# A key load in halves, mixer tiles in other rounds and a wait left out, in a gated attention and mixer decode kernel

## The chip, the core and the metric

One core of a Trainium2 chip runs the kernel. The metric is device microseconds of one execution, median of several runs. The core has a tensor engine (PE), a vector engine (DVE), a scalar engine (ACT), GpSimd (POOL) and a sync engine (SP), each with its own instruction stream; they wait for each other by semaphores. SP issues nearly all the loads here, into one queue that 16 DMA engines work off in order.

## What is computed

One token is decoded. Its 16 query heads, in groups of two, attend over 8 cached key and value heads of 65536 positions and 256 channels; beside this a small token mixer (a layer norm and an MLP with tanh GELU) runs on the same token, and a sigmoid gate mixes the two results. All tensors are bf16.

```python
def _A_ref(x, k_cache, v_cache, wq, wo):
    q = (x @ wq).reshape(B, Sq, 16, 256) ...
    scores = jnp.einsum("bhqd,bhkd->bhqk", q, k) * (Dh ** -0.5)
    p = softmax(scores)
    return jnp.einsum("bhqk,bhkd->bhqd", p, v) ... @ wo
def _B_ref(x, w1, b1, w2, b2):
    h = layernorm(x)                                   # [1, 1, 448]
    u = gelu(jnp.einsum("bsd,sf->bdf", h, w1) + b1)    # [1, 448, 1792]
    return (jnp.einsum("bdf,fs->bds", u, w2) + b2).transpose(0, 2, 1)
g = sigmoid((x * gate_w).sum(-1, keepdims=True))
return g * a + (1 - g) * b
```

The key and value caches are 268 MB each and are read once.

## The kernel before

The cache is worked off in `NP` = 32 rounds, called pairs in the change's title: four rounds (`PPH`) for each of 8 key heads. A round covers 16384 positions: 8 MB of keys and 8 MB of values. It consists of 8 chunks (`BODY`) of 2048 positions; the first four (`DC`) lie in one half of the round's keys, the last four in the other. In what follows K5 and V5 are the keys and values of round 5.

**PE, one round** (loop at L515). It first finishes the running maximum of the round before (`maxima`, L382 and L384). Then come the keys (`keys`, L371): for chunk k, 16 transposes into PSUM (`kst`, L344), interleaved with the scores of chunk k-1 (L365). DVE copies the even quarters of `kst` out to `ktT` (L650), ACT the odd ones (L787); a chunk's transposes wait until the chunk before it is copied out (`sem_ev`, L342). Before chunk 0 PE waits for the round's keys (`sem_k`, L333), before chunk 4 for `sem_kb` and, in rounds 2 and 3 alone, for a second half that came as a load of its own (`sem_kc`, L336 to L338, each under an `If`). Before the keys of a round it also waits for `s_qc` (L527), which DVE raises each time that it has copied the query of a head to `qcur` (L713, L735). After the keys come the mixer's projection if a tile is ready (L538) and `values` (L401 on): the exponentials `pT` of the round before times its values, 128 matmuls at L396. So round j multiplies the values of round j-1 (round 2 skips this, rounds 0 and 1 use their own), and round index 32 does the last ones. Every fourth round a head is finished: cleared, turned and multiplied by its part of `wo` (L446, L457).

**DVE, one round** (L722): 8 chunk copies; every fourth round the end of a head (`finish_head`); the maximum (L656 to L679); and in rounds 0 to `FT` - 1 = 13 one of 14 mixer tiles (`mixer`, L625 to L643), twelve operations on 128 x 448 with ACT's tanh (L791) between them. At the end of a head DVE copies the next query (L735). Since an engine's stream runs in order, the mixer tile of round j stands before the chunk copies of round j+1.

**SP's queue** (L282 to L306). The keys have a ring of one and a half rounds, `kring`; the values have one buffer, `vbuf`. K of round j is issued when PE has transposed the first four chunks of round j-1 (`sem_tr`, L287). V of round j is issued when the values of the round before are multiplied (`sem_pv`), since it overwrites their buffer. Loads of a round are one DMA of 8 MB each, except those of the first rounds: K0, K2 and K3 come in halves. The last values, V31, come in five pieces: the first (56 of 128 slices, 3.5 MB) goes to a free part of `kring`, the others wait for the multiplication of V30 (L305); behind them stand two last loads of `wo`.

**The end** (`tail`, L415 on): the pieces are multiplied as they land, the last ones already turned; the head is divided, projected and written out.

Of the kernel before, what the change touches and what calls it, by code (L numbers as in the profile page):

```python
# [7 lines left out]
AF = mybir.ActivationFunctionType  # L8
# [4 lines left out]
def bass_gated_mix__gqa_block_cached__mixer_token_mlp__decode_kernel(  # L13
# [22 lines left out]
    REP = HQ // H  # L36
    F = B_w1.shape[1]
    FT = F // 128
# [10 lines left out]
    NC = H * NCPH  # L49
    BODY = 2 * DC  # L50
    NV = BODY * NT
    NP = NC // BODY
    PPH = NCPH // BODY
# [10 lines left out]
    LEAD = 2  # L64
# [12 lines left out]
    GC0 = 0.796875  # L77
    GC1 = 0.044677734375

    assert FT <= NP - PPH  # L80

    HV = NV // 2
# [10 lines left out]
    with ctx:  # L95
# [6 lines left out]
        def new_sem(name):  # L102
            return ctx.enter_context(nc.semaphore(name))
# [90 lines left out]

        sem_k = new_sem("sem_k")
        sem_kb = new_sem("sem_kb")
        sem_kc = [new_sem("sem_kc%d" % i) for i in range(2)]
        s_qc = new_sem("s_qc")
        sem_v = new_sem("sem_v")
        sem_vp = [new_sem("semvp%d" % i) for i in range(len(pieces))]  # L200
        sem_x = new_sem("sem_x")
# [50 lines left out]
        @block.sync  # L252
        def _(eng):
            def load_wo(g):
                w = A_wo[g * REP * DH:(g + 1) * REP * DH, :]
                eng.dma_start(wo_rows, w.rearrange("(p i) n -> p (i n)", i=2 * REP)).then_inc(sem_wo, 16)

            load_wo(0)
            eng.dma_start(wq_a.rearrange("p j n -> p (j n)"),
                          A_wq[0:WF * P, :].rearrange("(p j) n -> p (j n)", p=P)).then_inc(sem_wq, 16)  # L260
            eng.dma_start(wq_b, A_wq[WF * P:DM, :].rearrange("r (a n) -> (r a) n", a=2)
                          ).then_inc(sem_wq, 16)
            def load(dst, cache, j, n0, n1, at, sem):
                eng.dma_start(dst[:, at + n0:at + n1, :].rearrange("p n d -> p (n d)"), src(cache, j, n0, n1)  # L264
                              ).then_inc(sem, 16)

            load(kring, A_k_cache, 0, HV, NV, 0, sem_k)
            load(kring, A_k_cache, 0, 0, HV, 0, sem_kb)

            def load_v(j):  # L270
                if j == 0:
                    eng.wait_ge(s_q, 1)
                    eng.wait_ge(s_hb, 1)
                else:
                    eng.wait_ge(sem_pv, j)
                load(vbuf, A_v_cache, j, 0, NV, 0, sem_v)
                g, m = divmod(j, PPH)
                if m == 0 and 1 <= g < H - 1:
                    eng.wait_ge(s_proj, g)
                    load_wo(g)  # L280

            for j in range(NP):  # L282
                if j == LEAD + 1:
                    eng.wait_ge(sem_tr[NB - 1], BODY * LEAD)
                    load(kring, A_k_cache, j, HV, NV, HV, sem_kc[1])
                if j >= 1:
                    eng.wait_ge(sem_tr[NB - 1], BODY * (j - 1) + DC)  # L287
                if j == LEAD:
                    load(kring, A_k_cache, j, HV, NV, 0, sem_k)
                    load(kring, A_k_cache, j, 0, HV, 0, sem_kc[0])  # L290
                elif j == LEAD + 1:
                    load(kring, A_k_cache, j, 0, HV, HV, sem_k)
                elif j >= 1:
                    load(kring, A_k_cache, j, 0, NV, HV * (j % 2), sem_k)
                if j < LEAD:
                    load_v(j)
                elif j > LEAD:
                    load_v(j - 1)


            for (n0, n1), sem in zip(pieces, sem_vp):
                if n0 == 0:
                    eng.wait_ge(sem_tr[NB - 1], BODY * (NP - 1))
                elif n0 == NRING:
                    eng.wait_ge(sem_pv, NP - 1)  # L305
                load(kring if n1 <= NRING else vbuf, A_v_cache, NP - 1, n0, n1, 0, sem)  # L306
            eng.wait_ge(s_proj, H - 1)
            for h in range(REP):
                w = A_wo[(HQ - REP + h) * DH:(HQ - REP + h + 1) * DH, :]
                eng.dma_start(wo_sb[:, h, :], w.rearrange("(p j) n -> p (j n)", j=2)).then_inc(sem_wl[h], 16)  # L310
            eng.wait_ge(s_fin, NCG)
            eng.dma_start(out_ap, out_row[:, :]).then_inc(sem_out, 16)
            eng.wait_ge(sem_out, 16)
# [13 lines left out]
        def _(pe):  # L327
# [3 lines left out]
            def transposes(k, c, j, u16, x2):  # L331
                if k == 0:
                    pe.wait_ge(sem_k, u16)  # L333
                if k == DC:
                    pe.wait_ge(sem_kb, 16)
                    for i, sem in enumerate(sem_kc):  # L336
                        with pe.If(j == LEAD + i):
                            pe.wait_ge(sem, 16)  # L338

                def tiles(at):  # L340
                    for b in range(NB):
                        pe.wait_ge(sem_ev[b], c + 1)  # L342
                        for i in range(4):
                            ins = pe.transpose(kst[:, b, i * P:(i + 1) * P],  # L344
                                               kring_f[:, at + NT * (k % DC) + 4 * b + i, :], ident[:, :])
                        ins.then_inc(sem_tr[b], 1)

                if k < DC:
                    tiles(HV)
                else:  # L350
                    with pe.If(x2 == 0):
                        tiles(0)
                    with pe.Else():
                        tiles(NV)
# [153 lines left out]
            v_reg = pe.alloc_register("v_reg")  # L508
            pe.reg_mov(v_reg, 1)
            on = OrderedEngineSet([pe.engine])  # L510
            m_reg = pe.alloc_register("m_reg")
            pe.reg_mov(m_reg, 0)
            g_reg = pe.alloc_register("g_reg")
            pe.reg_mov(g_reg, 1)
            with nc.Fori(0, NP + 1, 1, engines=on, head_slot={pe.engine: 0}) as jj:  # L515
# [7 lines left out]
                with pe.If(j < NP):  # L523
                    c0 = pe.snap(j * BODY, min_val=0, max_val=NC)
                    u16 = pe.snap(j * 16 + 16, min_val=16, max_val=16 * NP)
                    pe.wait_ge(s_qc, g)
                    keys(c0, j, u16, pe.snap(x2_reg, min_val=0, max_val=NV))  # L527
                with pe.Else():
                    pe.wait_ge(s_mix, 1)
                    for q in range(NCG):  # L530
                        r = slice(32 * q, 32 * q + 1)
                        pe.matmul(prj[r, 0:WG], rest[r, :], brow[r, :], start=False, stop=True,
                                  skip_group_check=True)
                with pe.If(j > 0):
                    with pe.If(j < FT + 1):
                        pe.wait_ge(s_pb, pe.snap(j, min_val=1, max_val=NP))
                        for q in range(NCG):
                            pe.matmul(prj[32 * q:32 * q + 1, WG:2 * WG], w2cur[:, :],  # L538
                                      gu[:, q * WG:(q + 1) * WG], start=False, stop=True, skip_group_check=True)
# [19 lines left out]
        def _(vec):  # L559
# [150 lines left out]
            vec.wait_ge(s_q, 1)  # L710
            vec.tensor_copy(qT[:, :, :].rearrange("p a b -> p (a b)"), sps[:, 1, 0:2 * HQ])
            vec.drain()
            vec.tensor_copy(qcur[:, :, :], qT[:, :, 0:REP]).then_inc(s_qc, 1)  # L713
            vec.wait_ge(s_h, 1)
            vec.drain()
            vec.tensor_copy(bcast[:, :], prj[:, DM:DM + 3])
# [5 lines left out]
            with nc.Fori(0, H, 1, engines=on) as g:  # L722
                with nc.Fori(0, PPH, 1, engines=on) as m:
                    j = vec.snap(g * PPH + m, min_val=0, max_val=NP)
                    c0 = vec.snap(j * BODY, min_val=0, max_val=NC)
                    for k in range(BODY):
                        evacuate(k, c0 + k)
                    with vec.If(j > 0):
                        with vec.If(m < 1):
                            finish_head(g)  # L730
                    maxima(vec.snap(j + 1, min_val=1, max_val=NP), c0)
                    with vec.If(j < FT):
                        mixer(j)
                with vec.If(g < H - 1):
                    vec.tensor_copy(qcur[:, :, :], qT[:, :, bass.ds(vec.snap(q_reg, min_val=REP, max_val=HQ - REP), REP)]  # L735
                                    ).then_inc(s_qc, 1)
                    vec.reg_add(q_reg, q_reg, REP)
            vec.wait_ge(s_proj, H - 1)
            vec.tensor_copy(brow1, prj[:, WG:2 * WG])
# [11 lines left out]
        def _(act):  # L751
# [12 lines left out]

            pt_reg = act.alloc_register("pt_reg")
            act.reg_mov(pt_reg, DC)

            def weights(j1):
                act.wait_ge(s_mneg, j1)
# [11 lines left out]
            with nc.Fori(0, NP, 1, engines=OrderedEngineSet([act.engine])) as j:  # L781
                c0 = act.snap(j * BODY, min_val=0, max_val=NC)
                for k in range(BODY):
                    act.wait_ge(sem_qk, c0 + (k + 1))
                    for b in range(1, NB, 2):
                        act.wait_ge(sem_tr[b], c0 + (k + 1))
                        act.activation(ktT[:, k % KTB, b, :], kst_b[:, b, :], AF.Copy).then_inc(sem_ev[b], 1)  # L787
                weights(act.snap(j + 1, min_val=1, max_val=NP))
                with act.If(j < FT):
                    act.wait_ge(s_u, j + 1)  # L790
                    act.activation(z_b[:, :], z_b[:, :], AF.Tanh).then_inc(s_tanh, 1)  # L791
            act.wait_ge(s_proj, H)
            for q in range(1, NCG, 2):
                act.activation(out_row[:, q * WG:(q + 1) * WG], prj[32 * q:32 * q + 1, 0:WG], AF.Copy
# [29 lines left out]
```

## Time and profile before

| what | value |
|---|---|
| timed runs, median of 3 | 1280.04 us (1279.2 to 1280.3) |
| profiled execution | 1272.94 us |
| its span, first to last instruction | 1271.1 us |
| mean granted clock of PE | 0.844 |
| moved by DMA | 544.39 MB, mean 428 GB/s |

The page gives busy times and shares per engine, and a row of digits for 40 slices of the span. A row of the table of windows gives, for each engine, busy time and count of instructions (PE, weight loads, DVE, ACT, POOL), then the granted clock, the mean busy share of the DMA engines, and GB/s. A row of the timeline gives the start, the duration, engine, line, operation, tiles and, in brackets, how long the engine stood idle before it and what ended that. A row of the DMA issues gives the median time from issue to landing; each row that is shown was asked for in a window that holds the issue named in the text. The chain of waits lists start and duration of what led to the end; a DMA's piece there runs from its issue to its landing.

### The profile page before, as it was taken

What the parts mean: (1) busy time and instruction counts of PE and PEld (TensorE: products, weight loads), DVE (VectorE), ACT (ScalarE), POOL (GpSimd) and SP (SyncE); (2) the same over time, 40 slices, a digit from 0 to 9 for tenths busy, and PEclk for the clock granted to TensorE, in tenths of its full rate; (3) what the DMA queues carried; (4) which work ended last, traced back from release to release, by engine and by line L of the source; (5) the groups of instructions that cost most, each with busy time, mean ns of one, the idle gap of its engine ahead of it and who ended that gap; (6) DMA issues with size and microseconds to landing.
All of it is one profiled execution on the core that took longest, in us unless ns stands there. A gap on an engine that the chain in (4) does not pass through costs nothing.

```text
span 1271.1 us, 39820 instructions
## 1 busy us (share of the span) xinstructions
PE 964.5 (76%) x17201; PEld 887.8 (70%) x17201; DVE 497.3 (39%) x1125; ACT 544.5 (43%) x692; POOL 0.9 (0%) x7
## 2 busy tenths in 40 slices
PE   4778777888777697767888677976679866688766
PEld 3667767778766687766787666876668766678765
DVE  3434544444544435443334233343233433333422
ACT  2345543445533445433444334453334543345532
POOL 0000000000000000000000000000000000000000
PEclk9878887888877888878988779888789888788878
DMA  9999999999999999999999999999999999999996
GB/s 418 427 419 429 422 429 429 441 431 429 429 441 431 429 435 450 409 438 445 439 431 425 445 431 429 431 441 429 429 431 429 441 431 429 429 437 450 431 429 281
DMA packets 11911, 544.39 MB, mean 428 GB/s; under 512 B 1401, under 2 KB 1660, under 8 KB 2940
## 3 DMA queue, kind: packets, MB, share of 16 engines
q1 hardware_dynamic: 11810, 544.22, 99.2%
q8 instruction: 8, 0.13, 0.0%
q10 hardware_dynamic: 90, 0.01, 0.0%
q14 instruction: 3, 0.02, 0.0%
HBM read 544.22 MB, written 0.00 MB: 428 GB/s over the span
## 4 chain that ended last, share of the span: by engine, by line
DMA 58%; PE 37%; DVE 2%; issue 2%; DVEq 1%; SPq 0%; ACT 0%
DMA kring<-in_A_k_cache_dram 57%; PE kst L344 27%; PE sps L365 7%; PE acc L396 2%; DMA wo_sb<-in_A_wo_dram 1%; PE acc L446 0%; ACT z_b L791 0%; PE sps L384 0%; PE acc L389 0%; DVE ktT L650 0%; DVE z_b L631 0%; DVE z_b L635 0%; DVE wtmp L629 0%; DVEq L624 0%; SPq L264 0%
## 5 line engine op out<-in xcount | busy, mean ns | idle before, releaser
L344 PE MATMUL kst<-ident,kring 128*128 128x128 f32 x4096 | 563.6, 299 | 200.7 <-DMA kring<-in_A_k_cache_dram 169.3
L344 PEld LDWEIGHTS kst<-ident,kring 128*128 128x128 f32 x4096 | 511.4, 155 | 209.3 <-issue 200.2
L787 ACT ACTIVATE ktT<-kst 128x1024 bf16<-128x1024 bf16 x512 | 499.1, 1021 | 354.9 <-PE kst L344 354.8
L650 DVE COPY ktT<-kst 128x1024 bf16<-128x1024 bf16 x512 | 353.8, 692 | 451.0 <-PE kst L344 425.8
L365 PEld LDWEIGHTS sps<-qcur,ktT 128*128 128x128 bf16 x8192 | 238.1, 96 | 2.8 <-issue 0.2
L365 PE MATMUL sps<-qcur,ktT 128*128 128x2 bf16 x8192 | 236.9, 164 | 0.0
L396 PE MATMUL acc<-vbuf,pT 128*2 128x256 bf16 x4024 | 161.1, 336 | 3.7 <-issue 2.3
L396 PEld LDWEIGHTS acc<-vbuf,pT 128*2 128x2 bf16 x4024 | 112.3, 102 | 44.2 <-issue 4.7
L770 ACT ACTIVATE fade<-mdif 128x2 f32<-128x2 f32 x32 | 6.5, 203 | 298.8 <-DVE mdif L667 298.8
L661 DVE TENSOR_REDUCE mrow<-sps 2x1 f32<-2x128 f32 x32 | 8.9, 279 | 158.6 <-PE sps L382 158.6
L382 PE MATMUL sps<-ident,mcol 128*2 128x128 f32 x32 | 8.9, 279 | 28.9 <-issue 22.9
L384 PEld LDWEIGHTS sps<-mdiag,mones 2*128 2x128 f32 x64 | 10.9, 211 | 27.9 <-DVE mdiag L663 27.9
L774 ACT ACTIVATE pT<-sps,mneg 128x64 f32 x128 | 30.3, 334 | 0.0
L389 PE MATMUL acc<-pT,ones_sq 128*128 128x32 bf16 x256 | 11.9, 181 | 24.1 <-issue 20.7
L384 PE MATMUL sps<-mdiag,mones 2*128 2x2 f32 x64 | 13.6, 280 | 21.3 <-DVE mdiag L663 21.3
L791 ACT ACTIVATE z_b<-z_b 128x448 bf16<-128x448 bf16 x14 | 8.1, 576 | 48.1 <-DVE z_b L637 48.1
L382 PEld LDWEIGHTS sps<-ident,mcol 128*2 128x2 f32 x32 | 2.6, 80 | 36.9 <-issue 27.7
L389 PEld LDWEIGHTS acc<-pT,ones_sq 128*128 128x128 bf16 x256 | 8.7, 99 | 27.4 <-issue 23.8
L684 DVE COPY accs<-acc 128x288 f32<-128x288 f32 x8 | 3.7, 458 | 60.2 <-PE acc L396 60.2
L656 DVE TENSOR_REDUCE mcol<-sps 128x2 f32<-128x256 f32 x32 | 13.5, 422 | 35.0 <-PE sps L365 35.0
L679 DVE TENSOR_SCALAR acc<-acc,fader 128x256 f32<-128x256 f32 x32 | 15.8, 492 | 2.5
L666 DVE TENSOR_SCALAR mneg<-sps 128x2 f32<-128x2 f32 x32 | 5.1, 160 | 16.5 <-PE sps L384 16.5
(108 smaller groups left out, 170.8 us busy)
## 6 DMA issues: line engine op xcount, KB each, us to landing
kring<-in_A_k_cache_dram SPq DMA_DIRECT2D x6, 4096.0 KB, 23.8
kring<-in_A_v_cache_dram SPq DMA_DIRECT2D x1, 3584.0 KB, 37.0
wo_sb<-in_A_wo_dram SPq DMA_DIRECT2D x7, 448.0 KB, 25.9
vbuf<-in_A_wq_dram SPq DMA_DIRECT2D x1, 3072.0 KB, 10.4
vbuf<-in_A_v_cache_dram SPq DMA_DIRECT2D x1, 2560.0 KB, 8.7
vbuf<-in_A_v_cache_dram SPq DMA_DIRECT2D x1, 1024.0 KB, 10.8
vbuf<-in_A_v_cache_dram SPq DMA_DIRECT2D x1, 768.0 KB, 12.2
vbuf<-in_A_wq_dram SPq DMA_DIRECT2D x1, 512.0 KB, 11.1
```

The source lines that it names most:

```text
L344: ins = pe.transpose(kst[:, b, i * P:(i + 1) * P], kring_f[:, at + NT * (k % DC) + 4 * b + i, :], ident[:, :])
L365: ins = pe.matmul(sps[:, 0, 2 * (NT * k + nt):2 * (NT * k + nt) + 2], ktT[:, par, b, ntl * DH + dj:(ntl + 1) * DH:2], qcur[:, dj, :], star ...
L382: pe.transpose(mxT, mcol[:, :], ident[:, :]).then_inc(s_mT, 1)
L384: pe.matmul(mxB, mones[:, :], mdiag[:, :], start=True, stop=True).then_inc(s_mB, 1)
L389: pe.matmul(acc[:, DENC:SELC], ones_sq[:, :], pT[:, r, :], start=False, stop=(r == BODY - 1), skip_group_check=True)
L396: ins = pe.matmul(acc[o:o + REP, 0:DH], pT[:, r, 2 * nt:2 * nt + 2], buf[:, n, :], start=False, stop=False, skip_group_check=True)
L650: vec.tensor_copy(ktT[:, k % KTB, b, :], kst_b[:, b, :]).then_inc(sem_ev[b], 1)
L656: vec.tensor_reduce(out=mcol[:, :], in_=scores_all.rearrange("p (n hh) -> p hh n", hh=REP), axis=AX.X, op=ALU.max)
L661: vec.tensor_reduce(out=mrow[:, :], in_=mxT, axis=AX.X, op=ALU.max)
L679: vec.tensor_scalar(acc[:, 0:DENC], acc[:, 0:DENC], fader[:, :], None, op0=ALU.mult).then_inc(s_acc, 1)
L774: ins = act.activation(pT[:, bass.ds(p0, DC), hh:2 * NT:REP], scores_all.rearrange("p (a r n hh) -> p a hh r n", a=2, r=DC, hh=REP)[:, hal ...
L787: act.activation(ktT[:, k % KTB, b, :], kst_b[:, b, :], AF.Copy).then_inc(sem_ev[b], 1)
```

## The change

It has three parts. The last key load, K31, is issued as two DMAs of half a round each; the second has its own semaphore, for which PE waits before chunk 4 of round 31. The 14 mixer tiles are made in rounds 4 to 17 in place of 0 to 13, and PE and ACT count them with a register. The semaphore `s_qc` and PE's wait for it are gone; the first scores of a head still come after a chunk copy that stands behind the query's copy in DVE's stream. Beside these the count that the transposes wait for is held in one name, `done`, with the same instructions as before.

```diff
+    MIX0 = LEAD + 2
+    assert MIX0 + FT <= NP - PPH
...
-        sem_kc = [new_sem("sem_kc%d" % i) for i in range(2)]
-        s_qc = new_sem("s_qc")
+        sem_kc = [new_sem("sem_kc%d" % i) for i in range(3)]
...
                 elif j == LEAD + 1:
                     load(kring, A_k_cache, j, 0, HV, HV, sem_k)
+                elif j == NP - 1:
+                    load(kring, A_k_cache, j, 0, HV, HV, sem_k)
+                    load(kring, A_k_cache, j, HV, NV, HV, sem_kc[2])
                 elif j >= 1:
                     load(kring, A_k_cache, j, 0, NV, HV * (j % 2), sem_k)
...
                 if k == DC:
                     pe.wait_ge(sem_kb, 16)
-                    for i, sem in enumerate(sem_kc):
-                        with pe.If(j == LEAD + i):
+                    for p, sem in zip((LEAD, LEAD + 1, NP - 1), sem_kc):
+                        with pe.If(j == p):
                             pe.wait_ge(sem, 16)
+
+                done = pe.snap(c + 1, min_val=1, max_val=NC)
...
-                        pe.wait_ge(sem_ev[b], c + 1)
+                        pe.wait_ge(sem_ev[b], done)
...
-                    pe.wait_ge(s_qc, g)
                     keys(c0, j, u16, pe.snap(x2_reg, min_val=0, max_val=NV))
...
-                with pe.If(j > 0):
-                    with pe.If(j < FT + 1):
-                        pe.wait_ge(s_pb, pe.snap(j, min_val=1, max_val=NP))
+                with pe.If(j > MIX0):
+                    with pe.If(j < MIX0 + FT + 1):
+                        pe.wait_ge(s_pb, pe.snap(mix_reg, min_val=1, max_val=FT))
+                        pe.reg_add(mix_reg, mix_reg, 1)
...
-                    with vec.If(j < FT):
-                        mixer(j)
+                    with vec.If(j >= MIX0):
+                        with vec.If(j < MIX0 + FT):
+                            mixer(vec.snap(kt_reg, min_val=0, max_val=FT - 1))
                 with vec.If(g < H - 1):
                     vec.tensor_copy(qcur[:, :, :], qT[:, :, bass.ds(vec.snap(q_reg, min_val=REP, max_val=HQ - REP), REP)]
-                                    ).then_inc(s_qc, 1)
+                                    )
...
-                with act.If(j < FT):
-                    act.wait_ge(s_u, j + 1)
-                    act.activation(z_b[:, :], z_b[:, :], AF.Tanh).then_inc(s_tanh, 1)
+                with act.If(j >= MIX0):
+                    with act.If(j < MIX0 + FT):
+                        act.wait_ge(s_u, act.snap(mix_reg, min_val=1, max_val=FT))
+                        act.activation(z_b[:, :], z_b[:, :], AF.Tanh).then_inc(s_tanh, 1)
+                        act.reg_add(mix_reg, mix_reg, 1)
```

More of the change, by code (lines that the diff above doesn't have):

```diff
@@ L78, in bass_gated_mix__gqa_block_cached__mixer_token_mlp__decode_kernel @@
     GC1 = 0.044677734375
-    assert FT <= NP - PPH
+    MIX0 = LEAD + 2
+    assert MIX0 + FT <= NP - PPH
     HV = NV // 2
@@ L510, in _ @@
             on = OrderedEngineSet([pe.engine])
+            mix_reg = pe.alloc_register("mix_reg")
+            pe.reg_mov(mix_reg, 1)
             m_reg = pe.alloc_register("m_reg")
@@ L712, in _ @@
             vec.drain()
-            vec.tensor_copy(qcur[:, :, :], qT[:, :, 0:REP]).then_inc(s_qc, 1)
+            vec.tensor_copy(qcur[:, :, :], qT[:, :, 0:REP])
             vec.wait_ge(s_h, 1)
@@ L766, in _ @@
             act.reg_mov(pt_reg, DC)
+            mix_reg = act.alloc_register("mix_reg")
+            act.reg_mov(mix_reg, 1)
             def weights(j1):
```

## The prediction, made before the changed kernel was run

> **What bounds the kernel now.** I read the page first: engine shares and DMA rows.
>
> ```profile
> span 1271.1 us, 39820 instructions
> PE 964.5 (76%) x17201; PEld 887.8 (70%) x17201; DVE 497.3 (39%) x1125; ACT 544.5 (43%) x692; POOL 0.9 (0%) x7
> DMA  9999999999999999999999999999999999999996
> DMA packets 11911, 544.39 MB, mean 428 GB/s; under 512 B 1401, under 2 KB 1660, under 8 KB 2940
> ```
>
> The DMA engines are full in every slice but the last, and no compute engine is near full. So the span is a transfer time: 544.39 MB, plus whatever time the queue stood empty. Next I looked for the empty stretches, with the table by windows over 2.5 us pieces (last columns: granted clock, DMA share, GB/s).
>
> ```profile
> 600.00:1000.00 400.00, 310.80 (x5457) 287.85 (x5458) 144.28 (x305) 172.82 (x217) 0.00 (x0) 0.84 1.00 433
> 150.00:152.50 2.50, 2.50 (x49) 2.49 (x49) 1.38 (x2) 1.47 (x2) 0.00 (x0) 1.00 0.22 79
> 1247.50:1250.00 2.50, 1.95 (x52) 1.54 (x56) 0.27 (x2) 0.00 (x0) 0.00 (x0) 0.79 0.51 218
> 1250.00:1252.50 2.50, 2.50 (x56) 1.73 (x52) 0.00 (x0) 0.00 (x0) 0.00 (x0) 0.53 0.00 0
> ```
>
> The steady rate is 433 GB/s. Only two places fall far below it: about 150 us and 1249 to 1254 us. A packet counts where it starts, so the windows place the holes; landings size them.
>
> **The hole at 150 us.** From SP's timeline (start of issue), the DMA issues (us to landing) and the chain (start, us):
>
> ```profile
> 117.51 0.43 SPq L264 DMA_DIRECT2D vbuf<-in_A_v_cache_dram  x1
> vbuf<-in_A_v_cache_dram SPq DMA_DIRECT2D x1, 32.6
> 148.69 0.33 SPq L264 DMA_DIRECT2D kring<-in_A_k_cache_dram  x1
> kring<-in_A_k_cache_dram SPq DMA_DIRECT2D x1, 22.6
> 1156.74 27.68 DMA kring<-in_A_k_cache_dram
> 1194.90 28.23 DMA kring<-in_A_k_cache_dram
> ```
>
> The last two rows are the chain's key loads of rounds 30 and 31. They land at 1184.42 and 1223.13, 38.71 us apart, with one value load between: a full 8 MB load takes 19.35 us. V2 lands at 117.51 + 32.6 = 150.1 and K4, right behind it, at 148.69 + 22.6 = 171.3: 21.2 instead of 19.35. K4 was issued only 1.4 us before V2 landed, and **1.8 us** was lost. Why K4 was late, from the timeline:
>
> ```profile
> 132.87 3.57 PE L344 MATMUL kst<-ident,kring 128*128 128x128 f32 x16
> 134.69 0.34 DVE L625 TENSOR_SCALAR wtmp<-hbT,params 128x448 bf16<-128x448 bf16 x1 [0.18 <-issue]
> 138.67 0.39 DVE L643 TENSOR_TENSOR gu<-wtmp,z_b 128x448 bf16<-128x448 bf16 x1
> 140.12 3.36 PE L344 MATMUL kst<-ident,kring 128*128 128x128 f32 x16 [3.69 <-DVE ktT L650]
> ```
>
> Round 3's chunk 0 is transposed by 136.44, but DVE runs mixer tile 2 from 134.69 to 139.06 before it copies that chunk out, and PE waits 3.69 us. SP issues K4 only after round 3's fourth chunk.
>
> **The hole at the end.**
>
> ```profile
> 1215.35 0.38 PE L384 MATMUL sps<-mdiag,mones 2*128 2x2 f32 x2 [0.67 <-DVE mdiag L663]
> 1223.26 6.23 PE L344 MATMUL kst<-ident,kring 128*128 128x128 f32 x32 [7.54 <-DMA kring<-in_A_k_cache_dram]
> 1245.40 1.74 PE L365 MATMUL sps<-qcur,ktT 128*128 128x2 bf16 x64
> 1248.34 5.33 PE L396 MATMUL acc<-vbuf,pT 128*2 128x256 bf16 x128
> 1253.71 1.85 SPq L264 DMA_DIRECT2D vbuf<-in_A_v_cache_dram  x4
> 1213.57 0.33 SPq L264 DMA_DIRECT2D vbuf<-in_A_v_cache_dram  x1
> vbuf<-in_A_v_cache_dram SPq DMA_DIRECT2D x1, 28.9
> 1213.94 0.43 SPq L264 DMA_DIRECT2D kring<-in_A_v_cache_dram  x1
> kring<-in_A_v_cache_dram SPq DMA_DIRECT2D x1, 3584.0 KB, 37.0
> vbuf<-in_A_v_cache_dram SPq DMA_DIRECT2D x1, 2560.0 KB, 8.7
> ```
>
> PE waits 7.54 us for K31, runs its keys from 1223.26 to 1247.14 (23.9 us), then multiplies V30 until 1253.67; only then may SP overwrite V30's buffer with the rest of V31. V30 landed at 1242.5 and V31's first piece at 1250.9, so V30 sat ready for 5.8 us and then the queue ran dry. The next piece lands at 1262.4, 11.5 us later, for a transfer of 2560 of 8192 KB, 2560/8192 x 19.35 = 6.05: **5.4 us** dead.
>
> **The change part by part.** *Last key load in halves.* The bytes are the same, with one more issue of 0.33 us on SP, ahead of V30's by 18 us. The cost of a split shows in two earlier half loads that stand next to each other in the queue:
>
> ```profile
> 95.09 0.33 SPq L264 DMA_DIRECT2D kring<-in_A_k_cache_dram  x1
> kring<-in_A_k_cache_dram SPq DMA_DIRECT2D x1, 4096.0 KB, 25.9
> 117.14 0.33 SPq L264 DMA_DIRECT2D kring<-in_A_k_cache_dram  x1
> kring<-in_A_k_cache_dram SPq DMA_DIRECT2D x1, 4096.0 KB, 13.6
> ```
>
> They land at 121.0 and 130.7, 9.7 apart, half of 19.35: a split costs nothing. K31's first half so lands at 1223.1 - 9.7 = 1213.4. PE is free of the maxima at 1215.73, so the keys start there, 7.5 us sooner. Chunk 4 needs the second half (1223.1); eight chunks take 23.9 us, so it is asked for at about 1215.7 + 12 = 1227.7, and the added wait costs nothing (all of PE stands behind it, so a late half would cost its full lateness). The keys end at about 1215.7 + 23.9 = 1239.6. V30 lands at 1242.5, so the stall goes there: the next late thing is V30, 2.9 us of PE wait.
>
> The V30 multiplication then starts at 1242.6. Its length depends on the clock: 3.67 us at full clock, 5.95 cold.
>
> ```profile
> 162.19 3.67 PE L396 MATMUL acc<-vbuf,pT 128*2 128x256 bf16 x128
> 100.75 5.95 PE L396 MATMUL acc<-vbuf,pT 128*2 128x256 bf16 x128
> 227.01 22.88 DMA kring<-in_A_k_cache_dram
> ```
>
> SP can issue the next piece at 1246.3 to 1248.5, that is 4.6 to 2.4 us before V31's first piece lands (1250.9). How much lead is enough? K6, issued at 227.01, landed 22.88 later; a full load takes 19.35, so it had at most 3.5 us of lead, and the DMA row has no hole there. K4 with 1.4 lost 1.8. On a straight line between the two, a lead of 2.4 loses 0.9 and one of 3.5 or more nothing. I take today's 5.33 us (a lead of 3.1, a loss of 0.4): the tail gains 5.4 - 0.4 = **5.0 us**, bounds 4.5 and 5.4.
>
> Today's run of V30's matmuls is itself half cold: the granted clock is 0.53 in the window from 1250.00. The Trainium skill, "TensorE: Matmul & The Clock Gate", section "What's actually happening", says that the clock is halved after an idle window of about 3.4 us and comes back after a busy one; by it a wait of 2.9 us may leave V30's matmuls cold throughout, and the tail is worth 4.5. No run here shows a wait in just that place.
>
> What follows the pieces moves along: from the end of V30's matmuls to the first of V31's PE took 1253.67 to 1259.75, 6.1 us, and they then met a piece that had landed at 1262.4. Both ends move by 5 to 6 us, and the last output-weight load still closes the chain.
>
> ```profile
> 1259.75 3.07 PE L396 MATMUL acc<-kring,pT 128*2 128x256 bf16 x56
> 1256.10 12.52 DMA wo_sb<-in_A_wo_dram
> 561.92 5.81 PE L344 MATMUL kst<-ident,kring 128*128 128x128 f32 x32 [9.24 <-DMA kring<-in_A_k_cache_dram]
> 483.99 5.54 PE L344 MATMUL kst<-ident,kring 128*128 128x128 f32 x32 [6.58 <-DVE qcur L735]
> 149.85 1.96 PE L344 MATMUL kst<-ident,kring 128*128 128x128 f32 x16 [0.41 <-issue]
> ```
>
> *Mixer tiles at pairs 4 to 17.* Tile 2 leaves round 2, so K4 is issued 3.69 us sooner, at 145.0, with a lead of 5.1: the 1.8 us come back. Bounds: 0 (the hole moves to another load) and 1.8; I take **1.8**, because tile 3 leaves too and rounds 4 and 5 begin earlier than now. The four added tiles (rounds 14 to 17) cost nothing: PE there waits 9.24 us for keys (row at 561.92), which covers the 4.4 us of a tile. Without that cover a round would start up to 3.7 us late.
>
> *The wait on the copied query.* It held PE for 6.58 us before round 12 (the row at 483.99). Chunk 0's copy on DVE still stands behind the mixer and the query copy, so PE gains one chunk of transposes and then waits for the chunk's copy. All of it lies under full DMA: 0. The added branch on PE stands beside the two that now precede chunk 4; the gap there is 0.41 us (row at 149.85), so one more is between 0 and about 0.4 us a round, as are those on DVE and ACT, and the same 9 us wait covers them: 0. In the last round the cover is the 2.9 us before V30.
>
> *Sum.* 1.8 + 5.0 = 6.8 us. The profiled execution took 1272.94 us (span 1271.1), so 1266.1; the median of the timed runs is 1280.04, 7.1 more, for which the profile shows no cause and which I leave as it is: **1273.2 us**.
>
> **The rivals.** *Tail alone:* the early hole is handed to a neighbouring load. For: leads in rounds 4 to 6 are short now (3.5 at K6). Against: PE starts those rounds sooner. Gain 5.0: 1275.0.
>
> *A split is not free:* behind each load the engines lose what they lost at K4, 1.8 us, and V30 and all behind it come that much later: 6.8 - 1.8 = 5.0, 1275.0. Against: the 9.7 us between halves. The Trainium skill, "DMA: Bandwidth & Descriptors", section "Anatomy of one DMA — SWDGE (gpsimd) path", gives each transfer a fixed cost of about 2.0 us beside its bytes, which would make it 1275.2; the spacing of the halves here disagrees for queued loads.
>
> *Early alone:* the halves land together, or PE has other work first, so the pieces stay late: 1.8, 1278.2. Against: PE had nothing between 1215.73 and 1223.26.
>
> *Nothing:* the timed runs end on something that the profile doesn't show: 1280.0.
>
> *Slower:* the mixer tiles in rounds 14 to 17 push the key issues too late. It decides once a round's lead (27.68 - 19.35 = 8.3 us at K30) falls under 3.5, which takes 4.8 us of lateness. A tile alone gives 3.7, a head change 6.6, so it needs lateness that adds up over rounds. If each of four rounds lost 3 us: 12 - 6.8 = 5.2 slower, 1285.2. Against: rounds 7 to 13 carry tiles today and the DMA row has no hole there.
>
> **How the numbers follow.** Forecast 0.66; tail alone 0.14; split not free 0.05; early alone 0.06; nothing 0.04; slower 0.05. The forecast's own range, 1.8 with 4.5 to 5.4, is 1272.8 to 1273.7. The timed runs spread from 1279.2 to 1280.3, and tail alone with its cold bound reaches 1275.5; as the 7 us between profiled and timed runs stay unexplained I add some 1.5 us at either end: 1271.0 to 1277.0. A measurement of this kernel can tell about 0.2%, 2.6 us, from no change. Forecast, tail alone and split give faster, 0.85; early alone (1.8 us) and nothing give the same, 0.10; slower 0.05.
>
> **What would show it.** Right: no 20 us window between 20 and 1230 us under 400 GB/s; K4 lands 19.4 us after V2; PE's first transposes of the last round wait for no DMA and start within 1 us of the maxima; V30's matmuls begin when V30 lands; the next piece lands 6 to 6.5 us after V31's first. Wrong: a new hole between 170 and 230 us or after round 14, a wait of PE at chunk 4 of the last round, or halves that land under 9 us apart or push V30 later than 29.5 us after K31's first half.

## The result, and the profile after

| | before | changed |
|---|---|---|
| timed runs, median | 1280.17 us (1279.2 to 1282.6) | 1266.04 us (1265.9 to 1266.4) |
| profiled execution | 1272.94 us | 1266.13 us |
| its span | 1271.1 us | 1264.3 us |

The ratio of the timed runs is 0.9887, with a 95% interval from 0.987 to 0.9904: 14.1 us faster, where 6.8 were forecast, and below the stated range (1271.0 to 1277.0). The two profiled executions differ by 6.8 us, the sum as forecast. The other 7.3 us lie in the kernel before, whose timed runs took 7.2 us more than its profiled one; the changed kernel's timed runs sit on its profile.

From the page of the changed kernel, the span and the DMA rows:

```profile
span 1264.3 us, 39978 instructions
DMA  9999999999999999999999999999999999999998
DMA packets 12055, 544.39 MB, mean 431 GB/s; under 512 B 1417, under 2 KB 1676, under 8 KB 2956
```

The same bytes in 6.8 us less of span. The hole at 150 us first: V2's and K4's issue in SP's timeline.

```profile
117.40 0.43 SPq L264 DMA_DIRECT2D vbuf<-in_A_v_cache_dram  x1
145.02 0.33 SPq L264 DMA_DIRECT2D kring<-in_A_k_cache_dram  x1
```

The same two in the view of DMA issues, the last number being the microseconds from issue to landing:

```profile
vbuf<-in_A_v_cache_dram SPq DMA_DIRECT2D x1, 33.1
kring<-in_A_k_cache_dram SPq DMA_DIRECT2D x1, 24.8
```

V2 lands at 150.5, K4 at 169.8, 19.3 apart: the hole is gone. K4 is issued at 145.02, where 145.0 was worked out, 5.5 us before V2 lands. The end, from PE's timeline of the changed kernel:

```profile
1214.71 0.38 PE L389 MATMUL sps<-mdiag,mones 2*128 2x2 f32 x2 [0.66 <-DVE mdiag L670]
1215.04 1.96 PE L349 MATMUL kst<-ident,kring 128*128 128x128 f32 x16
1226.43 1.96 PE L349 MATMUL kst<-ident,kring 128*128 128x128 f32 x16 [0.68 <-issue]
1241.04 5.33 PE L401 MATMUL acc<-vbuf,pT 128*2 128x256 bf16 x128 [1.88 <-DMA vbuf<-in_A_v_cache_dram]
```

SP's timeline there, and the DMA issues (KB each, and from issue to landing):

```profile
1213.61 0.33 SPq L264 DMA_DIRECT2D kring<-in_A_v_cache_dram  x1
1246.42 1.77 SPq L264 DMA_DIRECT2D vbuf<-in_A_v_cache_dram  x4
```

```profile
kring<-in_A_v_cache_dram SPq DMA_DIRECT2D x1, 3584.0 KB, 35.9
vbuf<-in_A_v_cache_dram SPq DMA_DIRECT2D x1, 2560.0 KB, 9.2
```

The last round's keys start right behind the maxima and wait for no DMA; at chunk 4 PE is idle for 0.68 us, for nothing that the profile shows, and not for the second half (before, with one branch less there, it was 0.41 in round 3). V30's matmuls now wait for V30 itself. V31's first piece lands at 1249.5, the next at 1255.6: 6.1 apart for a transfer of 6.05. That hole is gone too. Of the 6.8 us between the two profiled executions V31's first piece already shows 1.4 (1250.9 to 1249.5), the early part; the other 5.4 are the gap behind it, which shrinks from 11.5 to 6.1.

### The profile page after: what moved, and what is told of

Its sections match the earlier page's. It is cut to its first block, busy times and chain, and to the rows that moved or that the text cites. A ratio compares the mean times of both kernels' runs of the same rounds, so it can differ in the third digit from the quotient of the medians.

```text
span 1264.3 us, 39978 instructions
## 1 busy us (share of the span) xinstructions
PE 956.9 (76%) x17201; PEld 881.7 (70%) x17201; DVE 497.4 (39%) x1125; ACT 544.5 (43%) x692; POOL 0.9 (0%) x7
## 4 chain that ended last, share of the span: by engine, by line
DMA 63%; PE 34%; issue 1%; DVE 1%; DVEq 0%; SPq 0%; ACT 0%
DMA kring<-in_A_k_cache_dram 59%; PE kst L349 25%; PE sps L370 6%; DMA vbuf<-in_A_v_cache_dram 2%; PE acc L401 2%; DMA wo_sb<-in_A_wo_dram 1%; PE acc L451 0%; PE sps L389 0%; SPq L264 0%; PE acc L394 0%; DVE ktT L657 0%; PE sps L387 0%; ACT z_b L802 0%; DVE mrow L668 0%; DVE accs L691 0%
## 5 line engine op out<-in xcount | busy, mean ns | idle before, releaser
L349 PE MATMUL kst<-ident,kring 128*128 128x128 f32 x4096 | 557.2, 297 | 196.9 <-DMA kring<-in_A_k_cache_dram 173.1
L349 PEld LDWEIGHTS kst<-ident,kring 128*128 128x128 f32 x4096 | 505.5, 154 | 205.4 <-issue 199.9
L401 PE MATMUL acc<-vbuf,pT 128*2 128x256 bf16 x4024 | 158.3, 332 | 6.1 <-DMA vbuf<-in_A_v_cache_dram 3.4
L389 PE MATMUL sps<-mdiag,mones 2*128 2x2 f32 x64 | 14.1, 288 | 21.3 <-DVE mdiag L670 21.3
L394 PE MATMUL acc<-pT,ones_sq 128*128 128x32 bf16 x256 | 11.9, 182 | 22.8 <-issue 19.3
## 6 DMA issues: line engine op xcount, KB each, us to landing
vbuf<-in_A_wq_dram SPq DMA_DIRECT2D x1, 3072.0 KB, 10.3
```

Source lines behind the costliest of these rows:

```text
L349: ins = pe.transpose(kst[:, b, i * P:(i + 1) * P], kring_f[:, at + NT * (k % DC) + 4 * b + i, :], ident[:, :])
L389: pe.matmul(mxB, mones[:, :], mdiag[:, :], start=True, stop=True).then_inc(s_mB, 1)
L394: pe.matmul(acc[:, DENC:SELC], ones_sq[:, :], pT[:, r, :], start=False, stop=(r == BODY - 1), skip_group_check=True)
L401: ins = pe.matmul(acc[o:o + REP, 0:DH], pT[:, r, 2 * nt:2 * nt + 2], buf[:, n, :], start=False, stop=False, skip_group_check=True)
```

## The experiments

Theories A and B, told in the first expectation, are two answers to where the missing 7 us lay. Each kernel below is the one named with the edit shown, cut to its main lines; medians are of timed runs, the ratio is to the kernel before on the same chip. The executions of the kernel before fell mostly into two groups, and what follows is about these: on the chip that ran f1 to f4, 9 of 23 took 1271.5 to 1273.7 us and 14 took 1280.9 to 1282.4. I call them its short and its long course. The profile that the prediction was made from is of the short one, and all four timed executions behind the 1280.17 of the result are long ones.

**The kernel before again**

> The kernel before, unchanged, for the spread of its executions. Its one profiled execution took 1272.94 us and its timed runs 1279.2 to 1282.6, while the changed kernel's timed runs (1265.9 to 1266.4) sit on its profiled one (1266.13). Theory A (a loss that comes and goes in the kernel): executions near 1273 and near 1280 both appear, and a profile near 1280 shows holes in the DMA stream that the first profile lacks, most likely in rounds 2 to 6, where key loads were issued 1.4 to 4.3 us before the queue ran dry. Theory B (the profiled execution was the odd one, for a reason outside the kernel): all executions sit at 1280 and the DMA stream shows packets that are slower throughout, not holes.

1281.07 us (1272.98 to 1282.37). Of these eleven only the profiled one is short (1272.98, span 1271.2), which theory B would allow; but of 31 more executions of this kernel on the same chip 13 took 1272.3 to 1276.2, so B's "all executions sit at 1280" falls. The long course itself isn't in this profile.

**One part at a time**

```diff
 e1, to before
+                elif j == NP - 1:
+                    load(kring, A_k_cache, j, 0, HV, HV, sem_k)
+                    load(kring, A_k_cache, j, HV, NV, HV, sem_kc[2])
 e2, to before
-                    with vec.If(j < FT):
-                        mixer(j)
+                    with vec.If(j >= MIX0):
+                        with vec.If(j < MIX0 + FT):
+                            mixer(vec.snap(kt_reg, min_val=0, max_val=FT - 1))
 e3, to before
-                    pe.wait_ge(s_qc, g)
```

> The last key load in halves alone; mixer tiles and the wait on the query as before. Theory A: 5.0 us under before, about 1275 timed, 1268 where a profile has no early loss; the early loss stays. Theory B: the same 5.0 us. If instead the tail was what varied in the timed runs, this part alone brings 10 us or more, to about 1268.

1277.62 us over all ten executions: six from 1271.7 to 1280.3, for which the ratio is 0.997 (0.9935 to 1.0004), and four from 1291 to 1293, longer than any of the kernel before; no trace of these four is kept. The split alone doesn't narrow the spread, and there is no clear gain. The profiled execution (1272.34) shows why: V31's first two pieces land 6.1 us apart, as in the changed kernel, but K4 goes out 2.8 us after V2 has landed and lands 24.8 behind it, 5.4 more than its transfer takes. So the split does its work, and the early loss hides it.

> Mixer tiles in rounds 4 to 17 alone; last key load and the wait on the query as before. Theory A: the early loss goes whole, 1.8 us of it in the first profile and some 7 us more in the timed runs: about 1271 timed, and timed runs agree with the profile. Theory B: 1.8 us, about 1278.

1270.66 us (1269.18 to 1271.16), ratio 0.9941 (0.9917 to 0.9964), 9.2 us under the 1279.88 of before. One group, and the profile (1269.18) lies in it. Theory A holds and B falls: the early loss goes whole, and in the median execution it is some 9 us, not 1.8. Against the 13 short executions alone (median 1273.6) the gain is 3.0.

> The wait on the copied query left out alone; the rest as before. Both theories as forecast: nothing, within 1 us of before (1280), since the next chunk still waits for the copy that stands behind the query's on DVE. If the wait is what turns the early rounds from one course into the other, the timed runs fall to about 1273.

1281.15 us (1272.51 to 1282.74), ratio 1.0 (0.9968 to 1.0033): nothing, as forecast, and both courses are there (three of the ten are short).

**The wait put back, and the tiles moved by one round**

```diff
 f1, to the changed kernel
+                    pe.wait_ge(s_qc, g)
 f2 / f3, to the changed kernel
-    MIX0 = LEAD + 2
+    MIX0 = LEAD          (f2: rounds 2 to 15)
+    MIX0 = LEAD + 1      (f3: rounds 3 to 16)
```

> The changed kernel with the wait on the copied query put back. Theory C (the gain is two parts: mixer tiles out of the first rounds, some 9 us, and the halves of the last key load, some 4.6 us; the wait is worth nothing): 1266 us, as the changed kernel. Rival: the wait adds a late round after the head changes, whose clock then stays low; then one or more executions show a hole in the DMA stream and the median is 2 us or more higher.

1266.91 us (1265.73 to 1267.56), within 1 us of the changed kernel, with ranges that overlap. Worth nothing that these runs can tell.

> The changed kernel with mixer tiles in rounds 2 to 15. Theory C with its cause (tile after round 2 makes PE wait some 3.7 us in round 3, the tensor clock stays at half for the following chunks, K4 is issued late): the loss is back, executions spread over some 9 us, median 1268 to 1276. Rival (each tile in rounds 0 to 3 costs its share of time): the loss is half back, but the executions agree with each other within 2 us.

1283.5 us (1271.43 to 1285.39): the loss is back, and larger than expected (1268 to 1276). Six of the ten lie at 1283.4 to 1285.4, so the rival's narrow half loss falls.

> The changed kernel with mixer tiles in rounds 3 to 16. Theory C with its cause: round 3 has no tile before it and K4 is in time; round 4 waits for K4's landing, which covers most of the tile: 1266 us, narrow. Rival (shares): 1268.

1267.1 us; five of six within 1265.8 to 1267.8, one at 1272.7. So of the four tiles that the change takes out of rounds 0 to 3, the one of round 2, which stands before round 3's chunk copies, is enough to bring the loss back, and with the one of round 3 the median is 1.1 us over the changed kernel's. That lies between the two forecasts, 1266 and 1268; it is f2 that tells against shares. The tiles of rounds 0 and 1 were not tried alone.

f2's profile was one of the long ones. Its windows (length, busy time of PE, PEld, DVE, ACT and POOL, granted clock, DMA share, GB/s):

```profile
140.00:160.00 20.00, 19.31 (x295) 18.97 (x294) 8.58 (x13) 11.85 (x12) 0.00 (x0) 0.82 0.88 370
180.00:200.00 20.00, 19.55 (x267) 19.25 (x266) 8.19 (x12) 10.98 (x12) 0.00 (x0) 0.71 0.88 367
220.00:240.00 20.00, 15.95 (x193) 15.64 (x194) 8.59 (x17) 10.21 (x11) 0.00 (x0) 0.66 0.75 308
270.00:280.00 10.00, 9.55 (x112) 9.33 (x111) 3.77 (x6) 4.79 (x5) 0.00 (x0) 0.65 0.79 315
```

A row of holes, one in each round from K4 to K9. With two smaller ones in round 10 they are the whole loss of this execution: K11 lands at 461.1 us (issued at 436.04, landed 25.1 later), in the changed kernel at 443.1 (415.45 and 27.6), 18.0 us apart, and the spans differ by 18.1. Why the row is longer here than in the kernel before was not tried. Round 7 shows how one hole makes the next, in PE's timeline:

```profile
298.84 1.96 PE L349 MATMUL kst<-ident,kring 128*128 128x128 f32 x16 [0.63 <-DMA kring<-in_A_k_cache_dram]
305.42 3.67 PE L349 MATMUL kst<-ident,kring 128*128 128x128 f32 x16 [4.62 <-DVE ktT L657]
309.79 3.65 PE L349 MATMUL kst<-ident,kring 128*128 128x128 f32 x16
314.13 3.65 PE L349 MATMUL kst<-ident,kring 128*128 128x128 f32 x16
```

The window of the last two of these chunks, SP's timeline with the following key load, and that load from issue to landing:

```profile
310.00:317.50 7.50, 7.50 (x64) 7.44 (x64) 2.60 (x4) 3.23 (x4) 0.00 (x0) 0.50 0.93 402
```

```profile
317.82 0.33 SPq L264 DMA_DIRECT2D kring<-in_A_k_cache_dram  x1
```

```profile
kring<-in_A_k_cache_dram SPq DMA_DIRECT2D x1, 22.0
```

Chunk 0 runs as the keys land, PE waits 4.62 us for the tile, and chunks 1 to 3 then run at a clock of 0.50, 3.65 us for 16 transposes in place of 1.95. The next key load is issued 19.0 us after the first of these transposes began, when the queue is about to run empty, and it needs 22.0 to land: 41.0 us a round against 38.7 that the transfers take. So the next round is late again, until a round comes in which the clock returns sooner: in round 8 it is back by chunk 3, in rounds 9 and 10 by chunk 2.

**Chunk 0 twice.** To tell the clock from the tile's own time, PE is given something to do where it waits: the 16 transposes of chunk 0 are made twice, into the same place, in the rounds that follow a tile. DVE's tile takes as long as before (4.37 us in round 2 of the kernel before, 4.38 in f2 and in g1).

```diff
 f4, to before (g1: the same to f2, in the rounds after its tiles)
+                if k == 0:
+                    with pe.If(j > 0):
+                        with pe.If(j < FT + 1):
+                            for b in range(NB):
+                                pe.wait_ge(sem_ev[b], c + 1)
+                                for i in range(4):
+                                    pe.transpose(kst[:, b, i * P:(i + 1) * P],
+                                                 kring_f[:, HV + 4 * b + i, :], ident[:, :])
```

> The kernel before, with chunk 0's 16 transposes done twice in rounds 1 to 14, so that PE works where it waits for the mixer tile; it adds 1.8 us of PE work at full clock (3.5 at half) to these rounds and takes none of the tile's time away. Theory C with the clock as the cause: round 3's chunks 1 to 3 run at full clock in nearly every execution (1.95 us per 16 transposes in place of 3.65), K4 is issued near 148 us, and the median falls from 1280 to 1271 to 1275. Rival (the tile's time alone makes K4 late, the clock is chance): median stays at 1280 or rises by the added work.

1276.63 us (1275.11 to 1278.45): the two courses have become one, 4.4 us under the 1281.04 of before, but above the 1271 to 1275 expected. Both groups of before lie outside this spread, one on either side: it is 3.7 us above the short course's median, and the long one is gone. The profiled execution bears out the clock and not the time: round 3's chunks 1 to 3 take 1.95 to 1.97 us each, but the round begins 3.6 us later than in the short course (136.49 against 132.87). So K4 goes out at 150.87 and not near 148, 1.1 us before V2 lands, and lands 20.8 us behind it: some 1.5 us lost, and at K5 some 1.8.

> The changed kernel with mixer tiles in rounds 2 to 15 (1283.5 us, up to six holes in a row) and chunk 0 transposed twice in the rounds that follow a tile. Theory C with the clock: PE keeps its clock through the wait, the chunks after it take 1.95 us instead of 3.65, the row of holes does not form: 1268 to 1273 us and executions within 3 us of each other. Rival (the tile's time makes the row of holes): the added 1.8 to 3.5 us a round makes it worse, 1284 or more.

1268.25 us (1266.78 to 1269.58), ratio 0.9927 (0.9898 to 0.9956): f2 with more PE work in each of 14 rounds is 15.2 us faster than f2 (on another chip, where the kernel before has the same two courses). Round 3 in PE's timeline, two rows of f2 and then four of this kernel:

```profile
138.95 3.67 PE L349 MATMUL kst<-ident,kring 128*128 128x128 f32 x16 [3.63 <-DVE ktT L657]
143.31 3.65 PE L349 MATMUL kst<-ident,kring 128*128 128x128 f32 x16
```

```profile
137.85 3.10 PE L349 MATMUL kst<-ident,kring 128*128 128x128 f32 x16
141.64 1.97 PE L349 MATMUL kst<-ident,kring 128*128 128x128 f32 x16 [0.69 <-DVE ktT L665]
144.25 1.95 PE L349 MATMUL kst<-ident,kring 128*128 128x128 f32 x16
146.84 1.95 PE L349 MATMUL kst<-ident,kring 128*128 128x128 f32 x16
```

The end of the tile that both wait for, in DVE's timeline, first f2 and then this kernel:

```profile
137.48 0.39 DVE L650 TENSOR_TENSOR gu<-wtmp,z_b 128x448 bf16<-128x448 bf16 x1
140.18 0.39 DVE L658 TENSOR_TENSOR gu<-wtmp,z_b 128x448 bf16<-128x448 bf16 x1
```

PE's idle wait shrinks from 3.63 us to 0.69, and the chunks after it run at 1.95 us. Chunk 1 starts at the same distance from the end of the tile, 1.08 us in f2 and 1.07 here, so the added work brings chunk 1 no nearer to the tile; what differs is how long chunks 1 to 3 take. From chunk 1's start to K4's issue it is 10.7 us in f2 (149.61) and 7.2 here (148.81). The rival, that the tile's time alone makes the row of holes, expected 1284 or more and falls.

**The long course of the kernel before**

> The kernel before, for a profile of its longer course (about 1281 us in 14 of 23 executions beside the last call). If one is caught, theory C expects holes at K4 and after it at K5, K6 and on, each of 2 to 5 us, and a half clock in the chunks before each late issue. If not, a copy of the first profile, 1273 us.

> The same as the look before it: about 1281 us with a row of holes, or about 1273 us with one small hole.

1283.24 and 1281.71 us, both of the long course. The first, by span and GB/s of the 40 slices on its page:

```profile
span 1281.4 us, 39820 instructions
GB/s 417 422 430 421 361 440 421 378 426 426 426 426 440 426 452 432 426 440 426 426 454 430 436 430 426 426 440 426 454 430 426 440 426 426 454 430 426 426 452 282
```

PE's timeline of its round 3, and four windows of it:

```profile
133.86 3.42 PE L344 MATMUL kst<-ident,kring 128*128 128x128 f32 x16
141.14 3.67 PE L344 MATMUL kst<-ident,kring 128*128 128x128 f32 x16 [3.86 <-DVE ktT L650]
145.50 3.65 PE L344 MATMUL kst<-ident,kring 128*128 128x128 f32 x16
149.85 3.65 PE L344 MATMUL kst<-ident,kring 128*128 128x128 f32 x16
```

```profile
142.50:145.00 2.50, 2.50 (x25) 2.43 (x24) 1.24 (x2) 1.18 (x2) 0.00 (x0) 0.50 0.97 419
145.00:147.50 2.50, 2.50 (x35) 2.50 (x32) 0.69 (x1) 0.87 (x1) 0.00 (x0) 0.50 0.97 419
147.50:150.00 2.50, 2.50 (x41) 2.44 (x40) 0.69 (x1) 1.83 (x2) 0.00 (x0) 0.50 0.13 52
150.00:152.50 2.50, 2.50 (x13) 2.50 (x14) 0.69 (x1) 0.82 (x2) 0.00 (x0) 0.50 0.00 0
```

SP's timeline with V2 and K4, and the two from issue to landing:

```profile
118.35 0.43 SPq L264 DMA_DIRECT2D vbuf<-in_A_v_cache_dram  x1
153.53 0.33 SPq L264 DMA_DIRECT2D kring<-in_A_k_cache_dram  x1
```

```profile
vbuf<-in_A_v_cache_dram SPq DMA_DIRECT2D x1, 33.4
kring<-in_A_k_cache_dram SPq DMA_DIRECT2D x1, 21.8
```

Chunk 2 of the same round in the short course, the execution that the prediction was made from:

```profile
144.13 1.95 PE L344 MATMUL kst<-ident,kring 128*128 128x128 f32 x16
```

PE's wait for the tile is 3.86 us, against 3.69 in the short course. But there the clock came back within chunk 1 and K4 was issued at 148.69; here chunks 1 to 3 all stay at half clock and K4 goes out at 153.53, 1.8 us after V2 has landed (118.35 + 33.4 = 151.75). K4 lands at 175.3, 23.6 us after V2: 4.2 us lost. The slices show further holes behind it, 378 GB/s in the eighth (some 224 to 256 us) as the plainest. Against the short course K4 lands 4.0 us later; from one key load's landing to the next K5 then adds 0.3, K6 3.3, K7 2.0 and K8 0.3. That makes 9.9 of the 10.3 us by which the spans differ (K8 at 313.07 + 24.1 = 337.2 and at 299.81 + 27.50 = 327.3). The hole that was expected at K5 is all but missing. The other profiled executions of the long course, those of g3, e3 and e1, show the same start: a clock of 0.50 from 142.5 to 150 us, and K4 issued at 152.2 to 153.2, after V2 had landed. In e0's, a short one, the clock is back within chunk 1 and K4 goes out at 148.95.

**The split once more**

```diff
 h1, to the changed kernel
-                elif j == NP - 1:
-                    load(kring, A_k_cache, j, 0, HV, HV, sem_k)
-                    load(kring, A_k_cache, j, HV, NV, HV, sem_kc[2])
```

> The changed kernel with the last key load whole again (mixer tiles in rounds 4 to 17, no wait on the query). Theory C: the hole at the end is back and nothing else; 3.5 to 5 us over the changed kernel, 1269.5 to 1271, and within 1 us of the kernel with the mixer tiles moved alone (1270.7), as the wait on the query is worth nothing. Rival (the two parts help each other, the split is worth more once the early rounds are in time, or the query wait is worth a few us by itself): 1268 or less, or 1272 or more.

1270.67 us (1269.69 to 1272.66), the same as the tiles moved alone (1270.66) and 4.6 us over the changed kernel. The split is worth 4.6, the wait on the query nothing, and the two parts add up: 9.2 + 4.6 = 13.8, where the whole change brought 14.1.

## Why the prediction was wrong

**What held.** The bound (a transfer time with two holes), the place of both holes and what made each were right, and so was the sum against the profiled execution: 1271.1 - 6.8 = 1264.3, which is the span measured. That it fits to the tenth is luck: the early part gave 1.4 there and the end 5.4, where 1.8 and 5.0 were forecast. It is luck too that K4 was issued at 145.02 as worked out; with the same tiles moved e2 has it at 142.42. The split gave 4.6 us in the timed runs and 5.0 were forecast. V30's matmuls took the 5.33 us assumed. The lead of the next piece was 1249.5 - 1246.4 = 3.1 us, the figure that the prediction gives (its own times make it 3.0), and lost less than 0.1 instead of the 0.4 from the straight line, so 3.1 us of lead is enough. By the rule of the Trainium skill, "TensorE: Matmul & The Clock Gate", section "What's actually happening", as the prediction applied it, those matmuls would have taken 5.95; they took 5.33, and the measurement decides. The wait before them was 1.88 us and not 2.9: the sums of the exponentials, which PE makes between a round's keys and its values (0.36 us, after 0.86 idle), stand in that gap, and the prediction left them out. Halves land 9.7 us apart (the split is free), the wait on the query and the tiles in rounds 14 to 17 cost nothing, as forecast.

**What failed** is one term and one step. The term is the early hole, put at 1.8 us from one K4 that was issued 1.4 us before V2 landed. It measures some 9 us in the median execution (e2: 9.2), because that one takes the long course; how large a median gain is depends on how many executions do, here 14 of 23 on one chip and 5 of 10 on another. The step is the last line of the sum: "for which the profile shows no cause and which I leave as it is". The 7.1 us between profiled and timed runs were not an offset; they were the same hole in its long course, and the mixer tiles' move removes them with the rest. Half of that could have been read from the rows that the prediction shows. K4's issue was 1.4 us from the edge, and round 3's chunk 0 took 3.57 us for 16 transposes, which is a half clock; had chunks 2 and 3 stayed like that, at 3.65 instead of 1.95, K4 would have come 3.4 us later, 2 us behind the landing. That the loss then repeats in later rounds couldn't be read there; f2's round 7 shows it.

**The rivals.** The split is not dear, the early hole isn't handed on, and nothing was lost in rounds 14 to 17. None of them named a kernel before that runs in two ways, which was the true alternative, and it lay on the far side of the forecast. "Nothing" came nearest, with something in the timed runs that the profile doesn't show, but had it outlast the change.

**What stays open.** Why the clock returns early in one execution and not in the next wasn't tried; the runs show only that it does, and that with PE at work through the wait it was back in time in the traces of f4 and g1. Open too are the four executions of e1 above 1291 us and the longer row of f2.

## What to carry to other kernels

If the timed runs lie further from the profiled one than they spread, that distance is a term of its own: look for a wait that is decided by a margin of a microsecond or two, and price it on both sides of the margin before calling the rest an offset. A stream of loads that is kept full by an engine's progress has a lead for each issue, the time from the issue to the landing of the load ahead, and every lead that is too short costs; here 3.1 us was enough, 1.4 lost 1.8, and -1.8 lost 4.2. Small work of one engine is best put where the others wait for data anyway: the same mixer tiles cost some 9 us in the median execution when they began in round 0, and when they began in round 4 the loads behind them landed without a hole.

## What the runs showed of the hardware

PE kept busy is not enough for the full clock. In the long course of the kernel before, PE was busy for all of the 10 us from 142.5 to 152.5 (2.50 of 2.50 us in each of the four windows shown above) with transposes and narrow score matmuls, and the granted clock stayed at 0.50. The Trainium skill, "TensorE: Matmul & The Clock Gate", section "What's actually happening", has the full clock return after one busy window of about 3.4 us; these windows disagree, if busy is read as the profile's busy time. And a wait of 4 to 5 us could cost more than itself: in f2's round 7 it was followed by three chunks at 3.65 us in place of 1.95, and giving PE 16 superfluous transposes to do in it, in each round after a tile, made the kernel 15.2 us faster.
